# The third block of batch 0 in split float16, beside two blocks in float32

## The chip, the cores and the metric

One core of a Trainium2 chip runs the whole program. The metric is the device time of one execution in microseconds; the median of several executions is given, and one more execution is recorded by the hardware profiler. An engine is named by its profile name where rows are read: PE is TensorE (PEld its weight loads), DVE is VectorE, ACT is ScalarE, POOL is GpSimd, SP issues the DMAs.

## The reference

Attention over 4 batches, 8 heads, 1152 keys and head size 64, with queries averaged in pairs (576 of them), then two dense layers. In short:

```python
q_pool = q.reshape(B, H, S // 2, 2, D).mean(axis=3)
scores = scale * np.matmul(q_pool, k.transpose(0, 1, 3, 2))
attn = np.exp(scores - np.max(scores, axis=-1, keepdims=True))
attn = attn / (np.sum(attn, axis=-1, keepdims=True) + 1e-09)
x = np.matmul(attn, v)            # 4 x 8 x 576 x 64, heads joined to rows of 512
h = x @ w_in                      # 512 -> 2048
g = np.where(h >= 1, h, np.where(h <= -1, 0.0, (h + 1) ** 2 / 4))
y = g @ w_out                     # 2048 -> 512
h2 = np.maximum(np.maximum(y @ w1, y @ w2), y @ w3)   # 512 -> 768, three times
out = h2 @ w_o2                   # 768 -> 512
```

## The kernel before

Most products are made in float16 with each operand as a high and a low part (hi, lo), three matmuls for one: hi x hi, hi x lo, lo x hi. `split` makes the parts, the high one on GpSimd and the low one on VectorE; `root_scale` and `norm` find the power of two that scales them.

The attention runs over 48 units: 4 batches x 3 blocks of 192 queries (`i`) x 4 pairs of heads (`p`). In this text unit n is the n-th of them, from 0, so units 0 to 11 are batch 0 and units 8 to 11 its third block. A unit has three tiles of 128 rows by 1152 keys (`who` 0 and 1 for the two heads, 2 for the remaining 64 rows of both). For each tile `soft` makes scores on TensorE (`qk`, line 352), their maximum on VectorE (366) and the exponential with its sum on ScalarE (367, 368). `turned` brings the probabilities into the transposed tile `pt`, and `av` multiplies `pt` with v one unit later; `shares` brings the row sums into place (lines 379 to 388).

`WHOLE(b, p)` at line 38 says which units stay in float32; it is true for all of batch 0. In a float32 unit `turned` transposes all three tiles on TensorE (line 404, nine transposes a tile) and ScalarE evicts each to `pt` (415, 417); `av` uses float32 matmuls (435) on a float32 v. In a split unit tiles 0 and 1 are cast by ScalarE (421), subtracted by VectorE (422) and transposed by a DMA from SP (423); only tile 2 goes over TensorE, evicted by ScalarE (410) and VectorE (411); `av` uses three times the matmuls in float16 (440).

The order on TensorE is written out by hand: `ORDER` is a list of words for a unit, one list for float32 units and one for split units. s is `soft` of a tile, t `turned`, r `shares`, a1 the `av` of the unit before, q `q_prep` of the next pair of units, d a step of the dense part, w a step that prepares w_in and w_out. The float32 list puts q ahead of the third tile and `av` behind the second t; the split list puts `av` ahead of the third tile and q behind it. Dense steps start with unit 6: in four words d there are two up steps (line 506) and one down step (532), the down step of a block running while the next block's up steps run, so there is none before unit 10. What the other engines do is put in order by the scheduler of the language, by program order and its own estimate of time; each engine then runs its own queue in order, SP included.

k and v of a batch are prepared by `k_steps` and `v_steps` in steps that `put` ties to units (`K1` and `V1`: around the last units of the batch before): a load by SP into one of two buffers (`nat`), a square sum on ScalarE (line 266), then `split`, and for k a transpose by DMA (283). In batch 0 the float32 v is loaded straight into one of the four `vhl` buffers. The rest of the program (two weights, the dense part that is left, the last two layers) follows when the attention is over.

## Time and profile before

| | us |
|---|---|
| median of three runs | 1231.83 (1231.8 to 1234.66) |
| profiled execution | 1239.84 |
| its span, first to last instruction | 1237.9 |

Busy in the span: TensorE 1077.9 us (87%), VectorE 857.5 (69%), ScalarE 696.8 (56%), GpSimd 302.9 (24%). The rows below are of the profiled execution. A busy time of TensorE is a modelled one, as its matmuls are pipelined; a wait is named by what came last.

The stretches used below are cut at the first score matmul of a unit: unit 5 starts at 146.89 us, unit 8 at 200.03, unit 9 at 216.19, unit 10 at 231.74, unit 11 at 258.97, unit 12 at 279.70, unit 17 at 361.21, unit 20 at 405.51, unit 23 at 454.61, unit 24 at 473.50, unit 29 at 557.82, unit 32 at 602.88, unit 41 at 753.18.

### The profile page before, as it was taken

To read this page: it belongs to the slowest core of one execution; us is meant where nothing else is said; L and a number is where in the kernel's file an instruction comes from. 1 tells how busy PE (TensorE), PEld (TensorE's weight loads), DVE (VectorE), ACT (ScalarE), POOL (GpSimd) and SP (SyncE) were. 2 spreads that over 40 slices of the span, in tenths; PEclk is the share of its full clock that TensorE was granted. 3 is DMA by queue.
4 is the path that set the end of the run, shared out by engine and by line. 5 is a ranking of instruction groups with operands and counts; after the bars stand their busy time and mean duration, and the time that the engine had idled before them with its cause. 6 is when DMAs were issued, how large, how long until landed. Compare 5 with 4: busy or idle time off the path is not lost.

```text
span 1237.9 us, 26735 instructions
## 1 busy us (share of the span) xinstructions
PE 1077.9 (87%) x11058; PEld 881.2 (71%) x11058; DVE 857.5 (69%) x1454; ACT 696.8 (56%) x1241; POOL 302.9 (24%) x306
## 2 busy tenths in 40 slices
PE   0456788899999987999988899998697999999998
PEld 0334567677788876888877788887696876767774
DVE  3988765657888888988888988886988652322220
ACT  3868676656667777667776677766453411122111
POOL 1310012323222344322234422221643020100000
PEclk9867889999999999999999999999899999999999
DMA  9963211446766688965588766547433220000001
GB/s 289 267 199 106 90 27 26 84 87 155 129 113 120 109 172 170 167 110 110 110 158 177 146 105 107 97 88 157 160 96 117 90 67 18 10 27 18 17 18 43
DMA packets 273753, 134.90 MB, mean 109 GB/s; under 512 B 229088, under 2 KB 256736, under 8 KB 272608
## 3 DMA queue, kind: packets, MB, share of 16 engines
q1 hardware_dynamic: 273632, 133.20, 48.5%
q8 instruction: 86, 1.41, 0.5%
q14 instruction: 35, 0.29, 0.1%
HBM read 62.39 MB, written 9.44 MB: 58 GB/s over the span
## 4 chain that ended last, share of the span: by engine, by line
PE 41%; DVE 17%; issue 7%; DMA 7%; ACT 6%; POOL 4%; SPq 2%; ACTq 0%; POOLq 0%; DVEq 0%
PE p L752 17%; PE po L769 5%; PE ph L506 5%; PE py L532 4%; DVE st L366 4%; DMA qn<-in_q_dram 3%; PE sc L352 3%; PE tr L404 3%; PE av L440 2%; DVE g L517 2%; DVE hl L422 2%; DVE t L514 2%; ACT pf L368 1%; POOL g L515 1%; ACT hl L421 1%
## 5 line engine op out<-in xcount | busy, mean ns | idle before, releaser
L352 PE MATMUL sc<-kst,qst 128*64 128x512 f16 (+3 forms) x1152 | 178.2, 347 | 62.6 <-DMA qst<-qpre 21.1
L532 PE MATMUL py<-g,wou 128*128 128x192 f16 x2304 | 201.1, 248 | 22.4 <-POOL g L515 7.8
L752 PE MATMUL p<-yh,wm 128*128 128x288 f16 x1728 | 216.0, 287 | 3.7 <-ACT py L536 2.7
L532 PEld LDWEIGHTS <-wou 128*128 128x128 f16 x2304 | 191.3, 99 | 31.8 <-issue 31.4
L506 PE MATMUL ph<-xh,win 128*128 128x192 f16 x2304 | 203.2, 249 | 4.9 <-ACT py L536 2.6
L366 DVE TENSOR_REDUCE st<-sc 128x1 f32<-128x1152 f32 x144 | 194.1, 1348 | 18.0 <-PE sc L352 17.8
L752 PEld LDWEIGHTS <-wm 128*128 128x128 f16 x1728 | 169.6, 98 | 49.6 <-issue 4.4
L506 PEld LDWEIGHTS <-win 128*128 128x128 f16 x2304 | 195.1, 99 | 7.5 <-issue 5.7
L368 ACT ACTIVATE pf<-sc,st,esc 128x1152 f32<-128x1152 f32 x144 | 188.7, 1311 | 4.5
L352 PEld LDWEIGHTS <-qst 128*64 128x64 f16 (+1 forms) x1152 | 85.6, 109 | 124.3 <-issue 56.9
L513 POOL TENSOR_TENSOR rl<-t,rl 128x384 f32<-128x384 f32 x96 | 103.7, 1083 | 185.3 <-DVE rl L512 185.3
L404 PE MATMUL tr<-ident,pf 128*128 128x128 f32 x648 | 98.9, 306 | 26.3 <-ACT pf L368 17.4
L422 DVE TENSOR_TENSOR hl<-pf,hl 128x1152 f16<-128x1152 f32 x72 | 104.3, 1449 | 22.7 <-ACT hl L421 22.6
L404 PEld LDWEIGHTS tr<-ident,pf 128*128 128x128 f32 x648 | 83.5, 161 | 40.9 <-ACT pf L368 24.8
L367 ACT ACTIVATE st<-st,esc 128x1 f32<-128x1 f32 x144 | 41.6, 289 | 119.0 <-DVE st L366 118.8
L760 ACT ACTIVATE h<-mx 128x288 f16<-128x288 f32 x48 | 21.2, 442 | 133.3 <-DVE mx L758 133.3
L757 DVE TENSOR_TENSOR mx<-p,mx 128x288 f32<-128x288 f32 x48 | 21.9, 456 | 106.3 <-PE p L752 105.7
L515 POOL TENSOR_SCALAR g<-t,dgs 128x384 f16<-128x384 f32 x96 | 70.7, 738 | 97.0 <-DVE t L514 91.4
L440 PE MATMUL av<-pt,vhl 128*64 128x192 f16 x1944 | 87.1, 247 | 2.7 <-DMA pt<-hl 2.7
L440 PEld LDWEIGHTS <-vhl 128*64 128x64 f16 x1944 | 79.3, 110 | 12.4 <-issue 8.5
L517 DVE SCALAR_TENSOR_TENSOR g<-t,dgs,g 128x384 f16<-128x384 f32 x96 | 74.2, 781 | 16.4 <-POOL g L515 16.2
L421 ACT ACTIVATE hl<-pf 128x1152 f16<-128x1152 f32 x72 | 83.4, 1159 | 0.9
(169 smaller groups left out, 1339.0 us busy)
## 6 DMA issues: line engine op xcount, KB each, us to landing
kn<-in_k_dram SPq DMA_DIRECT2D x16, 576.0 KB, 4.6
vn<-in_v_dram SPq DMA_DIRECT2D x16, 576.0 KB, 5.0
raw_m<-in_moe_w_dram SPq DMA_DIRECT2D x12, 768.0 KB, 5.1
raw_in<-in_moe_w_in_dram SPq DMA_DIRECT2D x8, 1024.0 KB, 5.4
qn<-in_q_dram SPq DMA_DIRECT2D x24, 256.0 KB, 4.0
raw_ou<-in_moe_w_out_dram SPq DMA_DIRECT2D x10, 512.0 KB, 4.6
qst<-qst SPq DMA_DIRECT2D x48, 96.0 KB, 2.2
y_d<-ys SPq DMA_DIRECT2D x48, 96.0 KB, 2.0
```

Source lines behind the costliest of these rows:

```text
L352: nc.tensor.matmul(sc[m0:m1, n0:n1], qst[b, i, p][who][:, var, m0:m1], ks[:, h, n0:n1], start=(var == 0), stop=(var == 1))
L366: nc.vector.tensor_reduce(out=m, in_=sc, axis=AX.X, op=ALU.max, negate=True)
L368: nc.scalar.activation(out=pf, in_=sc, func=AF.Exp, bias=nb, scale=e, accum_out=sums[b, i, p][:, who:who + 1])
L404: nc.tensor.transpose(tr[:, c * P:(c + 1) * P], pf[:, c * P:(c + 1) * P], ident)
L421: nc.scalar.activation(out=hl[:, 0], in_=pf, func=AF.Copy)
L422: nc.vector.tensor_tensor(out=hl[:, 1], in0=pf, in1=hl[:, 0], op=ALU.subtract)
L440: nc.tensor.matmul(acc[64 * h:64 * h + 64], vhl[b, p][:, vi, h, c, :], pt[:, h, pi * KT + c, :], start=(c == 0 and e == 0), stop=(c == KT ...
L506: nc.tensor.matmul(ph[:, a], win[:, wi, kt, ff * P:(ff + 1) * P], x[:, xi, kt], start=(kt == 0 and e == 0), stop=(kt == KD - 1 and e == 2))
L513: nc.gpsimd.tensor_tensor(out=rl, in0=t2, in1=rl, op=ALU.add)
L517: nc.vector.scalar_tensor_tensor(out=g[:, 1, fs, :], in0=t2, scalar=gs, in1=g[:, 0, fs, :], op0=ALU.mult, op1=ALU.subtract)
L532: nc.tensor.matmul(py, wou[:, ff // 2, wi, ff % 2, m * P:(m + 1) * P], g[:, gi, ff, :], start=(ff == 0 and e == 0), stop=(ff == NF - 1 and ...
L752: nc.tensor.matmul(ph[:, :NB2], wm[:, wi, i, kt, ff * P:(ff + 1) * P], yh[:, yi, kt, n0:n0 + NB2], start=(kt == 0 and e == 0), stop=(kt == ...
```

## The change

`WHOLE` takes the block instead of the pair and is true for the first two blocks of batch 0 alone. So units 8 to 11 follow the split way in `turned`, in `av` and in `ORDER`. Their v is needed in two parts: a new generator `v_again` loads each pair's v of batch 0 a second time, into a `nat` buffer, and splits it into a `vhl` buffer, with the scale found before. Its load is tied to the third tile of units 4 to 7 and its split to the first tile of units 6 to 9. As v of block 2 is now scaled, the factor `Uv` of each pair is written again in that block.

```diff
--- before.py
+++ after.py
@@ -35,7 +35,7 @@
 DEPTH = 1
 DENSE = 6
 POOL_KV = False
-WHOLE = lambda b, p: b == 0
+WHOLE = lambda b, i: b == 0 and i < 2
 ORDERED = {mybir.EngineType.PE}
 
 
@@ -285,7 +285,7 @@
 
     def v_steps(b, p):
 
-        if WHOLE(b, p):
+        if WHOLE(b, 0):
             vn = stk.tile([P, 2, KT, D], F32, tag="vhl", name=f"vn{b}_{p}")
             load_q.dma_start(out=vn, in_=v[b, 2 * p:2 * p + 2].rearrange("h (p c) d -> p h c d", p=P))
             yield
@@ -300,6 +300,15 @@
         vv = vhl[b, p].rearrange("p e a b c -> p e (a b c)")
         yield from norm(vn, vv[:, 0], 1, b, p, "v")
         split(vv[:, 0], vv[:, 1], vn.rearrange("p a b c -> p (a b c)"), sb[b][:, p, 1:2])
+        yield
+
+    def v_again(p):
+
+        vn = load(v, 0, p, "v")
+        yield
+        vhl[0, p] = stk.tile([P, 2, 2, KT, D], F16, tag="vhl", name=f"vhl0_{p}")
+        vv = vhl[0, p].rearrange("p e a b c -> p e (a b c)")
+        split(vv[:, 0], vv[:, 1], vn.rearrange("p a b c -> p (a b c)"), sb[0][:, p, 1:2])
         yield
 
     def q_prep(b, i, p):
@@ -395,7 +404,7 @@
         if who == 0:
             PT[b, i, p] = ptp.tile([P, 2, 2 * KT, NB], F16, tag="pt", name=f"pt_{b}_{i}_{p}")
         pt = PT[b, i, p]
-        if who == 2 or WHOLE(b, p):
+        if who == 2 or WHOLE(b, i):
 
             tr = place(f"tr{key}")
             rs = tr[:, KT * P:KT * P + 2 * P]
@@ -404,7 +413,7 @@
                 nc.tensor.transpose(tr[:, c * P:(c + 1) * P], pf[:, c * P:(c + 1) * P], ident)
             if who == 2:
                 R[b, i, p] = rs
-            if not WHOLE(b, p):
+            if not WHOLE(b, i):
                 tr = tr.rearrange("p (c h q) -> p h c q", c=KT, h=2)
                 hi, lo = pt[:, :, 0:KT, P:NB], pt[:, :, KT:2 * KT, P:NB]
                 nc.scalar.activation(out=hi, in_=tr, func=AF.Copy)
@@ -428,23 +437,23 @@
         pt = PT.pop((b, i, p))
         bank = psg.tile([P, 512], F32, tag="g1", name=f"av{b}_{i}_{p}")
         acc = bank[:, :NB]
-        if WHOLE(b, p):
+        if WHOLE(b, i):
             pt = whole(pt)
             for c in range(KT):
                 for h in HO:
                     nc.tensor.matmul(acc[64 * h:64 * h + 64], vhl[b, p][:, h, c, :], pt[:, h, c, :],
                                      start=(c == 0), stop=(c == KT - 1))
-        for c in range(0 if WHOLE(b, p) else KT):
+        for c in range(0 if WHOLE(b, i) else KT):
             for e, (vi, pi) in enumerate(((0, 0), (0, 1), (1, 0))):
                 for h in HO:
                     nc.tensor.matmul(acc[64 * h:64 * h + 64], vhl[b, p][:, vi, h, c, :], pt[:, h, pi * KT + c, :],
                                      start=(c == 0 and e == 0), stop=(c == KT - 1 and e == 2))
         if p == 0:
             xf[b, i] = xp.tile([P, KD, NB], F32, tag="xf", bufs=1, name=f"xf{b}_{i}")
-        if i == 0:
-            if p == 0:
+        if i == 0 or (b == 0 and i == 2):
+            if p == 0 and i == 0:
                 Uv[b] = small.tile([P, NPAIR + 3], F32, tag="Uv", bufs=3, name=f"Uv{b}")
-            if WHOLE(b, p):
+            if WHOLE(b, i):
                 nc.vector.tensor_scalar(out=Uv[b][:, p:p + 1], in0=u_in[:, p:p + 1], scalar1=1.0, scalar2=None,
                                         op0=ALU.mult)
             else:
@@ -578,6 +587,11 @@
                 put(t + x, kg)
             for x in (V1 if b else V0[p]):
                 put(t + x, vg)
+
+    for p in range(NPAIR):
+        again = v_again(p)
+        for x in (2, 6):
+            put(3 * ((2 - 1) * NPAIR + p) + x, again)
 
     def now(t):
         for gen in events.get(t, ()):
@@ -625,7 +639,7 @@
                 wdue -= 1
 
     for n, (b, i, p) in enumerate(units):
-        for word in ORDER[WHOLE(b, p)].split():
+        for word in ORDER[WHOLE(b, i)].split():
             attend(n, word)
     last = len(units)
     turned(*behind.pop((last - 1, 2)))
```

## Rows read from the trace of the kernel before

**Rows 1.** The page's chain that ended last: shares of the span by engine.

```profile
PE 41%; DVE 17%; issue 7%; DMA 7%; ACT 6%; POOL 4%; SPq 2%; ACTq 0%; POOLq 0%; DVEq 0%
```

**Rows 2.** Windows of units 8 to 12: length, busy by engine, clock, DMA.

```profile
200.03:216.19 16.16, 14.09 (x139) 11.26 (x138) 7.97 (x16) 11.20 (x19) 3.69 (x4) 1.00 0.03 7
216.19:231.74 15.55, 14.18 (x142) 11.56 (x140) 10.07 (x21) 10.34 (x18) 7.12 (x8) 1.00 0.20 46
231.74:258.97 27.23, 22.71 (x192) 18.31 (x191) 16.04 (x33) 14.96 (x27) 6.43 (x8) 0.81 0.53 112
258.97:279.70 20.73, 18.36 (x191) 15.73 (x190) 11.93 (x23) 11.83 (x21) 6.80 (x7) 1.00 0.54 78
279.70:297.46 17.76, 15.85 (x175) 13.66 (x173) 12.83 (x20) 12.58 (x23) 5.81 (x6) 1.00 0.55 135
```

**Rows 3.** Timeline of units 8 and 10: start, us, instructions, idle time before.

```profile
201.58 1.20 PE L404 MATMUL tr<-ident,pf 128*128 128x128 f32 x9 [0.40 <-ACT pf L368]
...
239.14 1.16 ACT L266 ACTIVATE kpre<-kn 128x1152 bf16<-128x1152 f32 x1 [2.38 <-DMA kn<-in_k_dram]
...
240.31 1.29 ACT L368 ACTIVATE pf<-sc,st,esc 128x1152 f32<-128x1152 f32 x1
...
241.74 1.37 PE L352 MATMUL sc<-kst,qst 128*128 128x512 f16 x6 [2.98 <-ACT pf L368]
...
243.16 2.18 PE L404 MATMUL tr<-ident,pf 128*128 128x128 f32 x9
```

**Rows 4.** Windows of units 8 to 16, 20 to 28 and 32 to 40.

```profile
200.03:361.21 161.18, 144.41 (x1569) 122.08 (x1568) 114.77 (x205) 103.66 (x187) 52.28 (x55) 0.97 0.54 102
405.51:557.82 152.31, 136.84 (x1685) 119.56 (x1683) 131.22 (x219) 107.39 (x198) 55.05 (x55) 0.99 0.76 146
602.88:753.18 150.30, 136.61 (x1683) 119.39 (x1682) 129.78 (x219) 107.34 (x198) 53.87 (x54) 0.99 0.71 137
```

**Rows 5.** Groups of instructions by line: busy us, mean ns of one, idle before.

```profile
L532 PE MATMUL py<-g,wou 128*128 128x192 f16 x2304 | 201.1, 248 | 22.4 <-POOL g L515 7.8 <-DVE xf L453 7.6 <-DVE g L517 7.0
...
L422 DVE TENSOR_TENSOR hl<-pf,hl 128x1152 f16<-128x1152 f32 x72 | 104.3, 1449 | 22.7 <-ACT hl L421 22.6
...
L404 PE MATMUL tr<-ident,pf 128*128 128x128 f32 x648 | 98.9, 306 | 26.3 <-ACT pf L368 17.4 <-issue 4.4 <-ACT R L388 3.0
L440 PE MATMUL av<-pt,vhl 128*64 128x192 f16 x1944 | 87.1, 247 | 2.7 <-DMA pt<-hl 2.7
...
L421 ACT ACTIVATE hl<-pf 128x1152 f16<-128x1152 f32 x72 | 83.4, 1159 | 0.9
...
L411 DVE TENSOR_TENSOR pt<-tr,pt 128x1152 f16<-128x1152 f32 x36 | 48.8, 1355 | 10.5 <-ACT pt L410 10.5
...
L435 PE MATMUL av<-pt,vn 128*64 128x192 f32 x432 | 40.1, 342 | 0.0
...
L415 ACT ACTIVATE pt<-tr 128x1152 f32<-128x1152 f32 x24 | 27.1, 1129 | 21.4 <-PE tr L404 21.3
```

**Rows 6.** DMA issues of the page: count, KB each, median us to landing.

```profile
vn<-in_v_dram SPq DMA_DIRECT2D x16, 576.0 KB, 5.0
...
pt<-hl SPq DMA_TRANSPOSE x72, 4.8
```

**Rows 7.** Groups by line: the split of v in later batches.

```profile
L246 DVE SCALAR_TENSOR_TENSOR vhl<-vn,sb,vhl 128x1152 f16<-128x1152 f32 x12 | 21.1, 1758 | 11.5 <-POOL vhl L245 11.4
...
L245 POOL TENSOR_SCALAR vhl<-vn,sb 128x1152 f16<-128x1152 f32 x12 | 15.8, 1319 | 42.4 <-ACT t L511 14.8 <-DVE Uv L451 11.5 <-PE ph L506 9.3
```

**Rows 8.** Windows of unit 5 and of units 23 and 24.

```profile
146.89:164.50 17.61, 11.65 (x91) 8.37 (x90) 12.17 (x22) 11.40 (x20) 2.77 (x3) 0.90 0.23 47
454.61:473.50 18.89, 15.62 (x193) 13.51 (x191) 15.47 (x28) 12.50 (x24) 7.89 (x7) 1.00 0.98 189
473.50:493.38 19.88, 15.79 (x192) 13.57 (x190) 18.22 (x32) 14.85 (x27) 9.86 (x8) 1.00 0.75 170
```

**Rows 9.** Timeline at the start: the early load of batch 1's first v.

```profile
37.89 0.37 SPq L260 DMA_DIRECT2D vn<-in_v_dram  x1
```

## The prediction

> **What bounds the kernel now.** I read the chain of waits first [rows 1]: TensorE carries 41% of it, VectorE 17%, and no other engine has as much. So the order on TensorE sets the end, and what VectorE and ScalarE do counts where TensorE waits for them. Then I cut the span at the first score matmul of each unit. A unit is one batch, block and pair of heads; units 8 to 11 are the third block of batch 0, the one that changes, and unit 12 still holds the last float32 output sum of unit 11.
>
> The windows of units 8 to 12 [rows 2] differ widely. Units 8 and 9 take 16.16 and 15.55 us with 14 us of TensorE work: they hold two up steps of the dense part but no down step yet. Units 10 and 11 hold one down step more. Unit 11 takes 20.73 us, 18.36 of them TensorE; unit 10 takes 27.23 at a granted clock of 0.81, though it holds the same work. The reader should see in the timeline of unit 10 [rows 3] why: ScalarE, which runs its queue in order, sits 2.38 us in front of the square of the next k until its load lands; the exponential behind it starts only at 240.31, TensorE idles 2.98 us, and its next nine transposes take 2.18 us. In unit 8 the same nine take 1.20 us [rows 3]. That is the half clock (1.2 of 2.4 GHz), and the loss against unit 11 is 27.23 - 20.73 = 6.5 us.
>
> The best guide to the changed kernel is in this trace already: at the starts of batches 2 and 3 the same work (k and v of the next batch prepared beside the last block) runs with the split form of the probabilities. Units 8 to 16 take 161.18 us, units 20 to 28 152.31 and units 32 to 40 150.30 [rows 4].
>
> **The change, part by part.** Four units change, 8 to 11.
>
> *TensorE.* Each loses 18 of its 27 float32 transposes. By their group [rows 5] one costs 98.9 / 648 = 0.153 us, so 2.75 us. The float32 output sum costs 40.1 / 12 = 3.34 us, the split one 87.1 / 36 = 2.42 [rows 5], so 0.92 less. Together 3.7 us a unit, 14.7 in all; a part of these averages is half clock, so it is an upper figure.
>
> *ScalarE.* Three evictions of 1.13 us go, two casts of 1.159 us come and one eviction, counted like those [rows 5]: 3.4 us against 3.4, no change.
>
> *VectorE.* Two subtractions of 1.449 us and one of 1.355 are added [rows 5]: 4.25 us a unit, 17.0 in all. VectorE was the engine with room in these windows (8 to 16 us busy, [rows 2]). With it, units 8 to 16 hold 114.8 + 17.0 = 131.8 us of VectorE, and the two later stretches hold 131.22 and 129.78 [rows 4]; so they are a fair picture of the load.
>
> *SP and the DMA.* Two DMA transposes a unit are added, eight in all; the 72 that exist land in a median of 4.8 us [rows 6]. They have from the exponential of unit n to the output sum in unit n+1 to do so, about one unit. Behind them on SP stand the q loads and the copies of transposed q. I cost them at nothing, covered by the up steps of the next unit; without that cover the output sum would wait the remainder of 4.8 us. The trace's rows speak against a page here: the Trainium skill ("VectorE: DVE Perf Modes", section "The three transpose paths") gives 1309 ns for one 128x128 block by DMA against 390 ns on TensorE. An estimate from that page for the 18 blocks of one such transfer is 23.6 us, 188 us for eight, which would make the kernel far slower. The 4.8 us of the row decides: the blocks are not done one after the other.
>
> *The second v.* Four loads of 576 KB (5.0 us to land, [rows 6]) and four splits, each 1.319 us on GpSimd and 1.758 us on VectorE [rows 7]. They are programmed in units 4 to 9, the splits from unit 6 on. A split waits for its v buffer, which the float32 v leaves after the output sum of the block before; GpSimd runs in order, so additions of q and the dense part's g steps queue behind that wait, and TensorE's down steps read g. What a split puts on the path lies between 0 and its whole 1.76 us, 0 to 7.0 for four; it can't be a gain, being added work. VectorE is busy less than 75% in units 5, 8 and 9 [rows 2, 8], so I take a quarter, 1.8 us. The fold of the scale into Uv in units 9 to 12 is one small VectorE instruction in place of another: nothing.
>
> *The load buffers.* Now the two buffers for raw k and v hold the first k and v of batch 1 early; that v's load issues at 37.89 us [rows 9]. After the change reloads take them, and the first k and v of batch 1 must wait for the splits of the third and the fourth reload, in units 8 and 9. Both are squared in units 9 and 10, one unit after; landing needs 5.0 us. I take 0, with the price of a miss under the rivals.
>
> *Sum.* Replacing units 8 to 16 by the mean of the two later stretches: 161.18 - (152.31 + 150.30) / 2 = 161.18 - 151.3 = 9.9 us gained. This contains the end of unit 10's stall: in units 23 and 24 [rows 8] the clock is 1.00 and each takes under 20 us. Less 1.8 for the splits. The later stretches have a down step in all units, units 8 and 9 have none; 48 matmuls of 201.1 / 2304 [rows 5] make 4.2 us, 8.4 for two, but VectorE (14 to 16 us with its additions) rather than TensorE will be longest there, so I count 1.0 of it, between 0 and 8.4. Gain 9.9 - 1.8 + 1.0 = 9.1 us. With the bounds of the splits and the down steps it is 3.9 to 18. TensorE's order is fixed by hand, and what follows unit 16 is unchanged, so the gain reaches the end whole. The profiled execution took 1239.84 us (span 1237.9), so 1230.7 by its own time; the median of the runs is 8.0 lower, 1231.83, which gives **1222.7 us**, own range 1214 to 1228.
>
> **Rivals.**
> 1. *The stall stays, or one like it comes.* TensorE has only about 14 - 3.7 = 10.4 us of work in units 8 and 9 of some 15.5, and unit 5, with 11.65 of 17.61 us, ran at a clock of 0.90 [rows 8]. If the clock falls there, or the square of the late k stays ahead of the exponential, 6.5 us come back: 9.1 - 6.5 = 2.6 gained, 1229.2. Against it: units 23 and 24 have the same loads and no drop. The Trainium skill ("TensorE: Matmul & The Clock Gate", section "HAM oscillation — how this bites in real kernels") says that an array waiting between bursts goes back to half clock and starts the next burst cold. Rows 3 agree (2.18 us after the wait); by that rule thinning TensorE's work is itself a risk.
> 2. *Slower: the ring of two load buffers.* The first k and v of batch 1 land too late, ScalarE stands in front of their squares as it does in unit 10 now, and TensorE falls to half clock each time. Each costs 6.5 us as in unit 10. With both new ones and the old one kept: 9.1 - 3 x 6.5 = -10.4, 1242.2. It turns slower from the second. Against it: one unit of lead, against 5.0 us to land. For it: SP and GpSimd run in order, so a late split delays the load.
> 3. *More than forecast.* Units 8 and 9 fall towards TensorE's own work and half of the 8.4 us counts: 9.9 + 4.2 = 14.1, 1217.7.
> 4. *Nothing to gain in ordinary runs.* The profiled execution is 8.0 us above the median. If that is unit 10's stall and the like, runs without a profile lack it, and VectorE's 17 us use up the rest: 0 to 2 us, 1231.
>
> **How the numbers follow.** Forecast 0.55, rival 1 0.20, rival 2 0.12, rival 3 0.08, rival 4 0.05. About 0.3% (3.7 us) is what a measurement of this kernel can tell from no change. Faster by more: forecast, rival 3 and a fifth of rival 1 (a cheaper stall), 0.67. Within it: the rest of rival 1 and rival 4, 0.21. Slower: rival 2, 0.12. The range leaves out rival 2 and the far end of rival 3: 1215 to 1232.
>
> **What would show it.** Right: units 8 to 16 in about 152 us, no window of them below a clock of 0.95, units 10 and 11 at 16 to 19 us, VectorE busy about 135 us in the stretch. Rival 1: a window of units 8 to 12 at 0.9 or below, with ScalarE waiting for a k or v load in front of it. Rival 2: two or three such waits. Rival 3: units 8 and 9 under 14 us. Wrong altogether: the stretch as long as before with the clock at 1.00, which would mean that VectorE took over what TensorE gave; or a loss after unit 16, which I took as unchanged.

## The result, and the profile after

The changed kernel takes 1239.6 us (median; 1235.92 to 1240.62) against 1231.8 for the kernel before, a ratio of 1.0057 with an interval of 1.0036 to 1.0077. It is slower; the forecast was 1222.7, and the range ended at 1232. In a second sitting the same compiled program (e7 below) took 1.0017 of the kernel before (1.0001 to 1.0034), so the loss is 0.2 to 0.6%. The profiled execution of the first sitting took 1238.76 us with a span of 1237.0.

The base first. The kernel before was run once more, unchanged (e1): 1234.35 us, ratio 0.9997, span 1232.3, while the execution in front of the prediction had a span of 1237.9. Below, "the kernel before" in a comparison by stretches is this second execution, which lies near its median. By it the change does this: units 0 to 5 +0.3 us, units 6 and 7 together **+7.7**, units 8 to 16 **-5.0**, units 17 to 46 -0.5, and +2.3 from unit 47 to the end, together +4.7. Executions of one program differ by some of this. Two of the runs below have edits that left the compiled order as it was, so that e6 is a third execution of the kernel before and e7 a second one of the changed kernel:

| us in units | kernel before, three executions | changed kernel, two executions |
|---|---|---|
| 0 to 5 | 162.8 to 164.5 | 163.1 and 164.7 |
| 6 and 7 | 33.3 to 35.5 | 41.2 and 38.0 |
| 8 to 16 | 159.7 to 161.6 | 154.7 and 154.3 |
| 17 to 46 | 476.8 to 479.1 | 476.3 and 477.3 |
| 47 to the end | 397.2 to 399.5 | 401.7 and 401.1 |

Three differences are larger than these spreads: units 6 and 7 are 2.5 to 7.9 us longer, units 8 to 16 are 5.0 to 7.3 us shorter, and the end is 1.6 to 4.5 us longer.

Windows of the changed kernel for units 6 to 12, in that order (start and end, length; busy time and instructions of TensorE, its weight load, VectorE, ScalarE, GpSimd; granted clock, DMA share, GB/s). The last five answer to [rows 2]:

```profile
163.09:186.22 23.13, 17.70 (x139) 13.69 (x138) 16.60 (x25) 16.74 (x24) 4.69 (x5) 0.78 0.11 34
186.22:204.27 18.05, 15.60 (x140) 12.37 (x138) 14.22 (x19) 10.82 (x19) 6.25 (x7) 0.91 0.28 76
204.27:217.22 12.95, 11.55 (x122) 9.33 (x121) 9.94 (x19) 8.51 (x16) 5.50 (x5) 1.00 0.37 90
217.22:234.16 16.94, 12.78 (x139) 10.68 (x139) 15.92 (x24) 11.38 (x21) 6.27 (x8) 0.90 0.55 125
234.16:257.33 23.17, 18.77 (x189) 16.27 (x189) 21.52 (x39) 16.47 (x28) 9.20 (x8) 0.85 0.76 157
257.33:273.83 16.50, 15.11 (x193) 13.37 (x191) 14.34 (x20) 10.33 (x20) 8.11 (x7) 1.00 0.97 203
273.83:295.50 21.67, 17.00 (x191) 14.86 (x190) 18.78 (x35) 15.35 (x27) 7.11 (x8) 0.92 0.79 160
```

Units 8 and 11 run at a clock of 1.00 in 12.95 and 16.50 us, against 16.16 and 20.73 in [rows 2]. Units 9, 10 and 12 are below it (0.90, 0.85, 0.92), and unit 12 has grown from 17.76 to 21.67 us. Unit 6, where the first of the new splits stands, takes 23.13 us at 0.78 (19.98 in the execution ahead of the prediction).

The same columns for the second execution of the kernel before: units 6 and 7 in one window, units 8 to 16, and unit 10.

```profile
162.84:196.29 33.45, 27.99 (x275) 22.49 (x274) 25.31 (x41) 27.86 (x42) 9.55 (x11) 1.00 0.09 22
196.29:355.99 159.70, 144.02 (x1569) 122.09 (x1568) 114.85 (x205) 102.20 (x184) 53.57 (x55) 0.97 0.51 103
227.38:254.75 27.37, 22.65 (x192) 18.34 (x191) 16.03 (x33) 15.05 (x28) 6.62 (x8) 0.81 0.53 112
```

Units 6 and 7 take 33.45 us there at a clock of 1.00. Unit 10 is as long as in [rows 2], so its stall belongs to the kernel and not to one execution.

The changed kernel's units 6 and 7 in one window, then units 8 to 16, 20 to 28 and 32 to 40, as in [rows 4]:

```profile
163.09:204.27 41.18, 33.30 (x277) 26.06 (x275) 30.82 (x44) 27.57 (x42) 10.94 (x12) 0.83 0.19 52
204.27:358.98 154.71, 133.96 (x1569) 116.07 (x1568) 135.07 (x222) 104.80 (x189) 58.07 (x57) 0.96 0.72 144
403.06:554.66 151.60, 136.32 (x1683) 119.30 (x1682) 131.94 (x219) 107.44 (x198) 56.24 (x55) 0.99 0.76 146
599.37:748.16 148.79, 136.02 (x1684) 119.35 (x1683) 131.10 (x219) 107.18 (x198) 52.79 (x54) 0.99 0.72 139
```

Units 6 and 7 take 41.18 us at 0.83. Units 8 to 16 fell from 161.18 (159.70 in the second execution) to 154.71, not to about 151; VectorE holds 135.07 us in it. The two later ones are what they were.

Groups by line and DMA issues of the changed kernel, which answer to [rows 5] and [rows 7] (busy us, mean ns of one; idle before):

```profile
L431 DVE TENSOR_TENSOR hl<-pf,hl 128x1152 f16<-128x1152 f32 x80 | 115.4, 1443 | 26.5 <-ACT hl L430 26.5
...
L413 PE MATMUL tr<-ident,pf 128*128 128x128 f32 x576 | 87.0, 304 | 33.1 <-ACT pf L377 21.8 <-issue 4.6 <-ACT R L397 4.4
L449 PE MATMUL av<-pt,vhl 128*64 128x192 f16 x2160 | 96.7, 247 | 3.9 <-DMA pt<-hl 3.9
...
L246 DVE SCALAR_TENSOR_TENSOR vhl<-vn,sb,vhl 128x1152 f16<-128x1152 f32 x16 | 27.5, 1720 | 8.0 <-POOL vhl L245 7.9
...
L245 POOL TENSOR_SCALAR vhl<-vn,sb 128x1152 f16<-128x1152 f32 x16 | 21.6, 1352 | 54.8 <-ACT t L520 23.0 <-PE ph L515 10.0 <-PE av L444 7.6
```

The DMA issues, as in [rows 6] (KB of each, median us to landing):

```profile
vn<-in_v_dram SPq DMA_DIRECT2D x20, 576.0 KB, 4.6
...
pt<-hl SPq DMA_TRANSPOSE x80, 4.7
```

A transpose, an output sum, a subtraction and a landing cost what they cost before. The split of v (lines 245 and 246) has four more instructions on each engine and nearly the same mean (1352 ns against 1319 on GpSimd, 1720 against 1758 on VectorE). What changed is where they stand.

**Where units 6 and 7 go.** The timeline of unit 6 in the changed kernel (start, us, engine, line, instruction, idle time before and what ended it) is one chain through four queues:

```profile
161.63 0.38 POOL L230 PARTITION_ALL_REDUCE U_ou<-um_ou  x1 [6.85 <-DVE um_ou L96]
...
168.81 1.22 POOL L245 TENSOR_SCALAR vhl<-vn,sb 128x1152 f16<-128x1152 f32 x1 [6.80 <-issue]
...
170.06 1.42 DVE L246 SCALAR_TENSOR_TENSOR vhl<-vn,sb,vhl 128x1152 f16<-128x1152 f32 x1 [2.24 <-POOL vhl L245]
...
171.40 1.28 DVE L148 SCALAR_TENSOR_TENSOR wou<-wou,s_ou 128x1024 f16<-128x1024 f32 x1
...
172.71 1.15 ACT L147 ACTIVATE wou<-wou,s_ou 128x1024 f16<-128x1024 f32 x1 [2.13 <-DVE wou L148]
...
173.77 0.56 ACT L520 ACTIVATE t<-ph,hh 128x384 f32<-128x384 f32 x1
...
174.23 0.32 ACT L396 ACTIVATE R<-tr 128x192 f32<-128x192 f32 x1
174.58 0.22 ACT L397 ACTIVATE R<-tr 64x64 f32<-64x64 f32 x1
...
174.85 2.18 PE L413 MATMUL tr<-ident,pf 128*128 128x128 f32 x9 [3.09 <-ACT R L397]
```

GpSimd starts the first half of pair 0's split at 168.81. VectorE has the second half at the head of its queue, and has been idle for 2.24 us when GpSimd is done. Behind it on VectorE stands a second half of the split of w_out (line 148, 171.40), for which ScalarE waits 2.13 us with the next first half (line 147); behind that stand ScalarE's copies of R; and TensorE waits 3.09 us for those and runs its nine transposes at half clock, 2.18 us as in the stalled unit 10 of [rows 3] against 1.20. In e7, the second execution, the chain is the same: GpSimd starts at 169.35, the waits are 2.71, 2.52 and 3.40 us, and the nine transposes take 2.18.

GpSimd's 6.80 us ahead of the split wait for nothing that the profile shows ("issue"). The instruction before it in GpSimd's queue is the partition all-reduce that finds the scale of w_out (line 230). Its own row lasts 0.38 us, but in all twenty traces of this document GpSimd starts nothing for at least 6.7 us after the end of a row of a partition all-reduce. The kernel before shows it too (7.12 us here, in e1, and 7.03 in the execution ahead of the prediction), where an addition of q comes next:

```profile
159.08 0.38 POOL L230 PARTITION_ALL_REDUCE U_ou<-um_ou  x1 [5.84 <-issue]
166.57 0.98 POOL L321 TENSOR_TENSOR qn<-qn 128x384 f32<-128x384 f32 x1 [7.12 <-issue]
```

So the compiler put the first split right behind an instruction that most likely holds GpSimd for about 7 us. No run moves the all-reduce, so this is argued from the rows and not tested.

### The profile page after: what moved, and what is told of

Same layout as the page of the kernel before. It is cut to its first block, busy times and chain, and to the rows that moved or that the text cites. A ratio compares the mean times of both kernels' runs of the same rounds, so it can differ in the third digit from the quotient of the medians.

```text
span 1237.0 us, 26819 instructions
## 1 busy us (share of the span) xinstructions
PE 1068.9 (86%) x11058; PEld 876.3 (71%) x11058; DVE 884.4 (71%) x1474; ACT 696.2 (56%) x1241; POOL 313.6 (25%) x310
## 3 DMA queue, kind: packets, MB, share of 16 engines
q8 instruction: 86, 1.41, 0.5%
## 4 chain that ended last, share of the span: by engine, by line
PE 44%; DVE 22%; DMA 10%; ACT 9%; issue 9%; POOL 4%; SPq 2%; ACTq 0%; POOLq 0%; DVEq 0%
PE p L766 17%; PE py L541 6%; DVE st L375 5%; PE po L783 5%; PE sc L361 5%; PE ph L515 4%; PE av L449 3%; PE tr L413 3%; DVE hl L431 2%; DMA qn<-in_q_dram 2%; DVE g L526 2%; ACT pf L377 2%; DMA kn<-in_k_dram 2%; DVE t L523 2%; ACT hl L430 2%
## 5 line engine op out<-in xcount | busy, mean ns | idle before, releaser
L541 PE MATMUL py<-g,wou 128*128 128x192 f16 x2304 | 207.4, 252 | 26.8 <-DVE xf L462 12.0
L541 PEld LDWEIGHTS <-wou 128*128 128x128 f16 x2304 | 197.4, 101 | 36.7 <-issue 35.6
L522 POOL TENSOR_TENSOR rl<-t,rl 128x384 f32<-128x384 f32 x96 | 108.7, 1135 | 172.5 <-DVE rl L521 171.7
L431 DVE TENSOR_TENSOR hl<-pf,hl 128x1152 f16<-128x1152 f32 x80 | 115.4, 1443 | 26.5 <-ACT hl L430 26.5
L413 PE MATMUL tr<-ident,pf 128*128 128x128 f32 x576 | 87.0, 304 | 33.1 <-ACT pf L377 21.8
L376 ACT ACTIVATE st<-st,esc 128x1 f32<-128x1 f32 x144 | 41.7, 289 | 128.8 <-DVE st L375 128.3
L413 PEld LDWEIGHTS tr<-ident,pf 128*128 128x128 f32 x576 | 73.4, 159 | 46.0 <-ACT pf L377 28.7
L449 PE MATMUL av<-pt,vhl 128*64 128x192 f16 x2160 | 96.7, 247 | 3.9 <-DMA pt<-hl 3.9
L449 PEld LDWEIGHTS <-vhl 128*64 128x64 f16 x2160 | 88.1, 110 | 14.6 <-issue 9.7
L430 ACT ACTIVATE hl<-pf 128x1152 f16<-128x1152 f32 x80 | 92.6, 1158 | 0.9
```

The costliest lines, as they stand in the source:

```text
L413: nc.tensor.transpose(tr[:, c * P:(c + 1) * P], pf[:, c * P:(c + 1) * P], ident)
L430: nc.scalar.activation(out=hl[:, 0], in_=pf, func=AF.Copy)
L431: nc.vector.tensor_tensor(out=hl[:, 1], in0=pf, in1=hl[:, 0], op=ALU.subtract)
L449: nc.tensor.matmul(acc[64 * h:64 * h + 64], vhl[b, p][:, vi, h, c, :], pt[:, h, pi * KT + c, :], start=(c == 0 and e == 0), stop=(c == KT ...
L522: nc.gpsimd.tensor_tensor(out=rl, in0=t2, in1=rl, op=ALU.add)
L541: nc.tensor.matmul(py, wou[:, ff // 2, wi, ff % 2, m * P:(m + 1) * P], g[:, gi, ff, :], start=(ff == 0 and e == 0), stop=(ff == NF - 1 and ...
```

## The experiments

All ratios are against the kernel before, run on the same chip in the same sitting. The quoted expectations name theories by letters and say in each what they hold.

**e1: the kernel before again.** No edit.

> The kernel before, unchanged, profiled a second time. Its first profiled execution took 1239.84 us, 8.0 above the median of its timed runs. Theory A (the 8 us were the stall of unit 10 and its half clock, which ordinary executions don't have): this profile has a span near 1230 and unit 10 takes at most 22 us at a clock of 0.95 or more. Theory B (unit 10's stall belongs to the kernel, the 8 us lay elsewhere): unit 10 takes 26 us or more here too, and the ratio is 1.000.

Measured: 1234.35 us, 0.9997 (0.9975 to 1.0019). Unit 10 is 27.37 us at 0.81 again.

**e2: v split from the copy on the chip, no second load.**

```diff
-        vn = load(v, 0, p, "v")
+        vn = vhl[0, p]
-        ... stk.tile([P, 2, 2, KT, D], F16, tag="vhl", name=f"vhl0_{p}")
+        ... stk.tile([P, 2, 2, KT, D], F16, tag="vhl", bufs=5, name=f"vhl0_{p}")
-        rb = tp.tile([P, 3, 64], F32, tag="rb", bufs=2, ...
+        rb = tp.tile([P, 3, 64], F32, tag="rb", bufs=1, ...
```

> The changed kernel without the second load of v: the split parts are made from the float32 v that is on chip, in a fifth v buffer (one row-sum buffer is given up for the room), so the two load buffers keep the first k and v of batch 1 as before. The same splits, the same units in split form. Theory C (the reload's hold on the two load buffers and its place in the queues cost the time): 4 to 8 us below the changed kernel, ratio 0.997 to 1.001. Theory D (the split form of units 8 to 11 itself gains nothing over ordinary executions of before, as VectorE and a thin TensorE take the gain): within 2 us of the changed kernel, ratio 1.004 to 1.008.

Measured: 1239.6 us, 1.0037 (1.0020 to 1.0054). Units 6 and 7 take 37.3 us, units 8 to 16 155.2, units 17 to 46 482.2 (476.8 in the kernel before). The whole is no faster without the second load, but it holds two further changes: pair 0's split now ran at 36.2 us already, and some 5 us were lost after unit 16, which e8 and e16 show too (484.5 and 483.1). They share with e2 the fifth v buffer and the row-sum buffer given up for it; which of the two costs this was not tested. What the second load costs is read from e12.

**e3: the second load and split alone.** Batch 0 stays float32 throughout; the second split goes into a spare buffer. The edit is to the kernel before.

```diff
+    def v_again(p):
+
+        vn = load(v, 0, p, "v")
+        yield
+        spare = hlp.tile([P, 2, 2, KT, D], F16, tag="hl", name=f"vhl0_{p}")
...
```

> The kernel before with the second load and the split of v added, into buffers whose content nothing reads; all of batch 0 stays in float32. Theory C: most of the loss is here, ratio 1.004 to 1.008, units 4 to 9 longer by 4 to 8 us in sum. Theory D: the four splits are 12 us of GpSimd and VectorE beside other work, ratio 0.999 to 1.002.

Measured: 1241.81 us, 1.0048 (1.0028 to 1.0069). Nothing holds these splits back: they run from 52.6 to 127 us, beside the work on w_in and w_out. Units 0 to 5 end at 171.1 us in place of 162.8, units 6 and 7 take 33.6. So the same loads and splits cost some 8 us where they meet the work on the weights, here earlier than in the changed kernel. The spare buffer is one of the ring `hl`, so a part of this may be the order of the other engines (see e13).

**e4: TensorE's order of batch 0 kept in the third block.**

```diff
-        for word in ORDER[WHOLE(b, i)].split():
+        for word in ORDER[b == 0].split():
```

> The changed kernel, with units 8 to 11 following the word list of the float32 units (q ahead of the third tile, the output sum at the end). Theory D with the order as its part (the split list puts the output sum before its DMA transposes have landed): 2 us or more below the changed kernel. Otherwise within 2 us, ratio 1.004 to 1.008.

Measured: 1237.77 us, 1.0017 (0.9997 to 1.0038). Units 6 and 7 41.7, units 8 to 16 155.5: as in the changed kernel. The two words of the order are not the cause. The ratio is below 1.0057, but it is that of the changed kernel in e7.

**e5: the split form alone.** No second load, no second split; the output sums of units 8 to 11 read two slices of the split w_in in place of v. e10, e12 and e14 do the same.

```diff
-    for p in range(NPAIR):
-        again = v_again(p)
-        ...
+        vs = vhl[b, p]
+        if b == 0 and i == 2:
+            vs = win.rearrange(...)[:, :4 * KT * D].rearrange(...)
```

> This kernel makes the third block of batch 0 split and transposed by DMA, but neither loads nor splits v a second time: the output sums of these four units read two slices of the split w_in in place of a split v (so these four results are not the reference's). Theory A (the second load and the v splits, which fall among the last splits of w_out in units 6 and 7, cost the time, and the split form itself gains): units 2 to 7 back at 108 to 111 us (116.1 in the changed kernel, 108.1 in the kernel before), units 8 to 16 at 152 to 155, the whole at 1224 to 1229 us. Theory D (VectorE and a thinner TensorE eat what the split form frees): units 8 to 16 at 158 or more, the whole at 1232 to 1236. Theory E (the order of ScalarE's and VectorE's queues, which the compiler chooses anew, costs time in places that the change does not touch): units 2 to 16 as in theory A, but 3 us or more lost after unit 16, the whole at 1230 to 1235.

Measured: 1235.77 us, 1.0008 (0.9984 to 1.0032). Units 8 to 16 take 154.5 us, as in the whole change, so the split form does gain 5 to 7 us there. But units 6 and 7 take 37.5 us, 2 to 4 more than in the kernel before, although nothing was added to them. ScalarE's queue shows why something moved: the square of batch 1's first k, the 57th of ScalarE's activations in the trace of the kernel before (91.4 us), is the 165th here (214.2 us); the expectations of e13 and e14 count it as place 53 and 159. Its target comes from the ring `hl`, and the casts of unit 8 take buffers of that ring first.

**e6 and e7: the square of the next k queued one tile later**, in the kernel before and in the changed one.

```diff
-K1 = (-2, 0, 2)
+K1 = (-2, 1, 2)
```

> The kernel before with one number changed: the square of each next batch's k is queued one tile later, one tile ahead of its split in place of two, so that its load has two tiles to land as v's has. If the stall of unit 10 is ScalarE standing on that load: unit 10 falls from 27.4 us to about 20 at a clock of 0.95 or more, units 8 to 16 from 159.7 to 152 to 155, the whole to 1225 to 1229 us. If the wait only moves to the square of v or to the split: unit 10 stays above 25 us or another unit takes it up, the whole at 1231 to 1235.

Measured: 1234.44 us, 1.0004 (0.9984 to 1.0023). The edit tested nothing: the square still ran at 234.91 us (234.86 in e1), behind a wait of 2.12 us (2.26), and every engine's trace has the same instructions in the same order as in the kernel before. The compiler places the square by its own reckoning.

> The changed kernel with the same one number changed. If the half-clock stretches that it keeps in units 9, 10 and 12 (16.9, 23.2 and 21.7 us) are ScalarE standing on late k loads: these three fall to 15 to 19 us each, units 8 to 16 from 154.7 to about 147 to 150, units 2 to 7 stay at 114 to 117, the whole falls from 1239.6 to 1232 to 1236 us. If they come from VectorE, which is busy 16 to 22 us in them: no change in units 8 to 16 (153 to 156), the whole at 1237 to 1241.

Measured: 1237.2 us, 1.0017 (1.0001 to 1.0034). Units 9, 10 and 12 take 17.2, 22.1 and 17.1 us (16.9, 23.2, 21.7), unit 11 takes 20.4 (16.5), and the stretch stays at 154.3. But here, too, the traces of ScalarE, VectorE, GpSimd and SP agree with the changed kernel's instruction by instruction, so neither theory was tested. What it shows is how far two executions of one program differ: units 9 and 10 have low clocks again, the third falls into unit 11 in place of 12, and units 6 and 7, one window each, take 38.0 us in place of 41.2:

```profile
164.70:185.53 20.83, 16.21 (x140) 12.92 (x138) 15.58 (x20) 14.57 (x22) 4.67 (x5) 0.84 0.10 31
185.53:202.71 17.18, 14.02 (x139) 11.25 (x138) 13.29 (x21) 11.36 (x18) 6.24 (x7) 1.00 0.29 79
```

**e8: e2 with the splits queued behind those of w_out.**

```diff
-        for x in (2, 6):
+        for x in (2, (12, 10, 8, 7)[p]):
```

> The kernel without reload (v split from the copy on the chip, 1239.6 us, units 2 to 7 in 112.3, units 8 to 16 in 155.2) with the four v splits queued later: all from the first tile of unit 8 on, behind the last splits of w_out, in place of one in each of units 6 to 9. Theory A (collision with the splits of w_out): units 6 and 7 fall to 15.6 to 18 us each, units 2 to 7 to 108 to 109, units 8 to 16 rise by 2 us at most, the whole at 1234 to 1237 us. Theory E (the order chosen anew costs the time, wherever the splits stand): units 2 to 7 change by less than 2 us, or what they give is lost elsewhere; the whole at 1238 to 1242.

Measured: 1240.63 us, 1.0040 (1.0017 to 1.0063), units 6 and 7 38.3. It tested nothing, as e6: the splits ran at 168.6 and 186.2 us all the same, and the order on ScalarE, VectorE, GpSimd and SP is that of e2, of which this is a second execution.

**e9 to e11: ScalarE's and VectorE's order kept as programmed**, in the kernel before, in e5 and in the changed kernel.

```diff
-ORDERED = {mybir.EngineType.PE}
+ORDERED = {mybir.EngineType.PE, mybir.EngineType.Activation, mybir.EngineType.DVE}
```

> The kernel before with ScalarE's and VectorE's instructions, too, kept in the order in which the program issues them (as TensorE's already are), up to the last layers. It is the base for the next two runs; only its difference to them counts. All theories: the order in which the program is written puts the work on the weights at the end of each unit, so units 0 to 7 get longer, the whole somewhere between 1235 and 1290 us; unit 10 shows whether a stall on the load of k is there as well.

> As the run before, but with the third block of batch 0 split and transposed by DMA (no second load or split of v; two slices of the split w_in stand in for the split v, so these four results are not the reference's). Theory E (the split form alone gained nothing in the whole because the compiler chose a new order for ScalarE and VectorE, which cost some 3 us in units 2 to 7): with the order kept, units 2 to 7 agree with the fixed kernel before within 1 us, units 8 to 16 are 4 to 8 us shorter, and the whole is 4 to 8 us shorter than that kernel. Theory F (units 2 to 7 vary between executions, order or not, and the gain in units 8 to 16 is that of the late stall): the whole within 2 us of that kernel, or units 2 to 7 differ by 2 us or more at the same order.

> The whole change (second load and split of v with it) with ScalarE's and VectorE's order kept as programmed. Theory E: units 2 to 7 rise over the two fixed kernels only by what the reload itself does, at most the four splits of 1.76 us on VectorE (0 to 7 us), and the whole lies 0 to 6 us below the fixed kernel before. Theory C (what hurts is that the second loads take the two load buffers from the first k and v of batch 1): units 8 to 12 show ScalarE or VectorE waiting for late k or v loads, and units 8 to 16 gain less than in the run before by 3 us or more; the whole is as long as the fixed kernel before or longer.

Measured: 2051.8, 2074.0 and 2078.6 us (1.6635, 1.6815, 1.6852). The base left the range that was meant, and at this order the split form lengthens units 8 to 16 from 274.6 to 301.9 us. Nothing follows for the tuned kernel but that the order of these two queues is worth 800 us of it, so an edit that moves it is not a local one. Units 2 to 7 agree within 1.3 us between the first two.

**e12: second loads without splits.** One column of each load is read in place of its split.

```diff
-        split(vv[:, 0], vv[:, 1], vn.rearrange(...), sb[0][:, p, 1:2])
+        nc.vector.tensor_scalar(out=one, in0=vn[:, 0, 0, 0:1], scalar1=1.0, ...)
```

> The split form of the third block with the second loads of v in their place, but with one column of each read in place of its split (the split w_in stands in for the split v, so four results are not the reference's). It lies between the split form alone (1235.8 us, units 2 to 7 in 112.5) and the whole change (1239.6, 116.1). Theory C (the loads' hold on the two buffers costs the time): units 2 to 7 at 115 to 117, the whole at 1238 to 1240 us. Theory A' (the splits do it, on GpSimd and VectorE among the last splits of w_out): units 2 to 7 at 111 to 113.5, the whole at 1234 to 1237 us.

Measured: 1229.78 us, 0.9969 (0.9945 to 0.9992): faster than the kernel before. Against the changed kernel only the splits are gone (and the order that goes with them), and units 6 and 7 take 34.13 us in place of 41.18 (38.01 in e7), at a clock of 0.95 in place of 0.83, while units 8 to 16 stay at 154.5. The window of units 6 and 7:

```profile
158.59:192.72 34.13, 29.66 (x276) 23.59 (x274) 27.05 (x44) 28.62 (x44) 10.19 (x11) 0.95 0.13 30
```

So in units 6 and 7 the second loads cost next to nothing; the splits do, or the order that goes with them, which differs here in many rows before unit 8. That the whole is faster than the kernel before comes in good part from elsewhere: units 0 to 5 take 158.6 us (162.8 in e1).

**e13: the moved square alone, in the kernel before.** Two buffers of the ring `hl` are taken in unit 8.

```diff
+                if key in ((8, 0), (8, 1)):
+                    pin = hlp.tile([P, 2 * KT * D], F16, tag="hl", ...)
+                    nc.vector.tensor_scalar(out=pin[:, 0:1], in0=item[4][:, 0:1], ...)
```

> The kernel before with one thing of the change alone: in unit 8 two buffers of the ring hl are taken (one column of the probabilities is copied into each), as the split form's casts take them. ScalarE's square of the first k of batch 1, which takes a buffer of that ring too, can then no longer run ahead in unit 2 and moves behind unit 8 (from place 53 of ScalarE's queue to place 159), and the compiler orders the rest anew, up to unit 7 nearly as in the split form alone. Theory E (this new order costs the time in units 2 to 7): units 2 to 7 in 111.5 to 114 us in place of 108.1, the whole at 1237 to 1241 us. Rival (units 2 to 7 vary by themselves): the whole within 2 us of the kernel before in the same session, units 2 to 7 at 107.5 to 111.

Measured: 1235.09 us, 1.0013 (0.9993 to 1.0033). The window of unit 6 of e5:

```profile
162.97:182.82 19.85, 16.67 (x139) 13.10 (x138) 14.34 (x22) 15.91 (x24) 4.13 (x4) 0.83 0.04 9
```

And of e13:

```profile
162.22:182.08 19.86, 16.68 (x140) 13.11 (x138) 14.27 (x21) 15.93 (x24) 4.13 (x4) 0.83 0.05 10
```

Units 2 to 6 of the two agree within 0.1 us, though e13 has no split form at all: the order before unit 8 is set by this one square. Units 6 and 7 take 36.4 us in e13, 3.0 more than in e1 and 0.9 more than in the execution ahead of the prediction, and units 8 to 16 give 2.1 of it back. The whole is not told from no change, so the size of this effect stays open.

**e14: the split form with the square put back** (the first k of batch 1 loaded and squared five tiles earlier).

```diff
-            for x in (K1 if b else K0[p]):
+            for x in ((-5, -4, 2) if b == 1 and p == 0 else K1 if b else K0[p]):
```

> The split form alone (no second v; the split w_in stands in for the split v, so four results are not the reference's), with the first k of batch 1 loaded and squared five tiles earlier in the program, ahead of unit 8's casts: the square is back at place 53, and ScalarE's order is that of the kernel before up to the last splits of w_out. Theory E: units 2 to 7 back at 107.5 to 110 us (112.5 without this), units 8 to 16 at 153 to 155.5, the whole at 1228 to 1232 us, faster than the kernel before by 0.2 to 0.5%. Rival (the split form gains nothing even so): the whole at 1233.5 to 1237 us.

Measured: 1232.99 us, 0.9984 (0.9961 to 1.0006). It can't be told from e5 (1.0008; the intervals overlap), and the stretches are not those of theory E: units 6 and 7 fell only from 37.5 to 35.8, and units 8 to 16 rose to 157.5.

**e15: the second split on GpSimd alone.**

```diff
-        split(vv[:, 0], vv[:, 1], vn.rearrange(...), sb[0][:, p, 1:2])
+        nc.gpsimd.tensor_scalar(out=vv[:, 0], in0=x, scalar1=s, ...)
+        nc.gpsimd.tensor_scalar(out=x, in0=x, scalar1=s, ...)
+        nc.gpsimd.tensor_tensor(out=vv[:, 1], in0=x, in1=vv[:, 0], op=ALU.subtract)
```

> The whole change with the second v split on GpSimd alone (its second half by a scaling in place and a subtraction there, nothing on VectorE). ScalarE's order stays that of the changed kernel but for a row or two, VectorE's too but for the four steps taken out. Theory A' (the VectorE half of the splits stands among the last splits of w_out and the dense steps in units 6 to 8): units 6 and 7 together fall from 41.2 to 36 to 38.5 us, units 2 to 7 to 111.5 to 114, the whole from 1239.6 to 1233 to 1236.5 us. Rival (what a split costs is the change of order, not VectorE's time): units 6 and 7 at 40 to 42 us, the whole at 1237.5 to 1241. Third case: GpSimd's longer steps hold up the dense part's g steps behind them; units 8 to 10 get longer by 2 us or more, 1240 or above.

Measured: 1246.47 us, 1.0106 (1.0065 to 1.0146). The order on ScalarE is the changed kernel's but for a few rows, VectorE is relieved of its halves, and units 6 and 7 rise to 43.4. So VectorE's time for its half is not what a split costs. The timeline of unit 6:

```profile
169.49 1.22 POOL L312 TENSOR_SCALAR vhl<-vn,sb 128x1152 f16<-128x1152 f32 x1 [7.54 <-PE ph L518]
...
172.11 2.37 POOL L314 TENSOR_TENSOR vhl<-vn,vhl 128x1152 f16<-128x1152 f32 x1
...
174.45 0.99 POOL L525 TENSOR_TENSOR rl<-t,rl 128x384 f32<-128x384 f32 x1
...
175.47 0.56 DVE L526 SCALAR_TENSOR_TENSOR t<-t,rl 128x384 f32<-128x384 f32 x1 [5.97 <-POOL rl L525]
...
177.26 1.15 ACT L147 ACTIVATE wou<-wou,s_ou 128x1024 f16<-128x1024 f32 x1 [4.89 <-DVE wou L148]
...
178.44 1.13 ACT L427 ACTIVATE pt<-tr 128x1152 f32<-128x1152 f32 x1
...
179.62 2.13 PE L364 MATMUL sc<-kst,qst 128*64 128x512 f16 x12 [5.99 <-ACT pt L427]
```

The dense part's addition (line 525) stands behind the three steps of the split on GpSimd until 174.45; VectorE waits 5.97 us for it, with the split of w_out (line 148) behind; ScalarE waits 4.89 us for that; TensorE waits 5.99 for ScalarE's eviction. It is the chain of the changed kernel with a longer first link; GpSimd starts 7.54 us after the all-reduce here.

**e16: copy on the chip, GpSimd alone, square early**, the three edits above in one kernel.

> All that theories E and A' ask for, as a complete kernel: v split from the copy on the chip (fifth v buffer, no second load), on GpSimd alone, and the first k of batch 1 loaded and squared five tiles earlier. If E and A' hold: units 2 to 7 in 107.5 to 110 us, units 8 to 16 in 153 to 156; units 20 to 28 may keep the 3.7 us that the fifth buffer cost in the kernel without reload; the whole at 1229 to 1234 us. If they don't: 1236 to 1241.

Measured: 1239.43 us, 1.0041 (1.0020 to 1.0061). Units 6 and 7 take 34.6 us, but units 2 to 5 78.3 (74.6 in e1) and units 17 to 46 483.1, a price that e2 shows as well.

**e17 and e18: the second split without GpSimd**, its first half on ScalarE (e17) or both halves on VectorE (e18). Load, place in the program and all else are the changed kernel's.

```diff
-        split(vv[:, 0], vv[:, 1], vn.rearrange(...), sb[0][:, p, 1:2])
+        split_rows(vv[:, 0], vv[:, 1], vn.rearrange(...), sb[0][:, p, 1:2])      # e17
+        nc.vector.tensor_scalar(out=vv[:, 0], in0=x, scalar1=s, ...)             # e18
+        nc.vector.scalar_tensor_tensor(out=vv[:, 1], in0=x, scalar=s, in1=vv[:, 0], ...)
```

> The whole change with the first half of the four v splits on ScalarE instead of GpSimd (the second half stays on VectorE). The queues of ScalarE and VectorE keep their order but for a few places. Theory H (VectorE stands in front of the split's second half until GpSimd, whose queue runs in order, has done the first, and the splits of w_out, ScalarE's evictions and TensorE stand behind that): units 6 and 7 together fall from 41.2 to 36 to 38.5 us, the whole from 1239.6 to 1232 to 1236 us. Rival (it is the added work beside the splits of w_out, whoever does it; ScalarE is as full there): units 6 and 7 at 39.5 us or more, the whole at 1237 to 1243.

Measured: 1235.05 us, 1.0013 (0.9998 to 1.0027). Up to the end of unit 6 ScalarE and VectorE have the changed kernel's order, with the one row added on ScalarE. Units 6 and 7, one window each, 33.63 us together (its profiled execution, 1239.8, lies above its median; the rest of it is not read):

```profile
164.04:180.64 16.60, 13.87 (x139) 11.26 (x138) 15.20 (x18) 15.31 (x23) 3.48 (x4) 1.00 0.13 40
180.64:197.67 17.03, 13.96 (x139) 11.25 (x138) 13.87 (x22) 12.58 (x21) 4.08 (x5) 1.00 0.26 72
```

> The whole change with both halves of the four v splits on VectorE. It takes GpSimd out too, but adds some 1.3 us a split to VectorE, and moves more of the order (44 rows of ScalarE, 114 of VectorE). Theory H: units 6 and 7 at 36.5 to 39 us, the whole at 1233 to 1237. Rival (added work on an engine that is full beside the splits of w_out): units 6 and 7 at 40 us or more, the whole at 1238 to 1244.

Measured: 1231.13 us, 0.9978 (0.9957 to 0.9999). It is complete and the fastest of the complete kernels. Units 6 and 7, 33.74 us together:

```profile
163.82:179.81 15.99, 13.96 (x139) 11.25 (x138) 14.58 (x20) 13.31 (x21) 4.55 (x4) 1.00 0.14 44
179.81:197.56 17.75, 15.58 (x139) 12.38 (x138) 16.61 (x27) 13.53 (x22) 6.79 (x6) 0.90 0.24 67
```

Both bring units 6 and 7 from 41.18 us (38.01 in e7) to 33.6 and 33.7, what they take in e1, with the same two splits in them. Nearly all of it comes in unit 6: 23.13 and 20.83 us in the changed kernel, 16.60 and 15.99 here. Unit 7, where the second split stands, hardly differs (18.05 and 17.18 against 17.03 and 17.75). What ScalarE waits for ahead of the first halves of w_out's split shows it, first in the groups by line of the changed kernel:

```profile
L147 ACT ACTIVATE wou<-wou,s_ou 128x1024 f16<-128x1024 f32 x7 | 8.0, 1144 | 5.8 <-DVE wou L148 5.8
```

Then in the groups by line of e18, with its own two halves of v:

```profile
L147 ACT ACTIVATE wou<-wou,s_ou 128x1024 f16<-128x1024 f32 x7 | 8.0, 1145 | 0.0
...
L313 DVE SCALAR_TENSOR_TENSOR vhl<-vn,sb,vhl 128x1152 f16<-128x1152 f32 x4 | 5.6, 1409 | 0.0
...
L312 DVE TENSOR_SCALAR vhl<-vn,sb 128x1152 f16<-128x1152 f32 x4 | 3.5, 870 | 0.0
```

5.8 us of waiting for VectorE are gone, though VectorE now does both halves; in e17 1.2 us are left, and the kernel before has 1.4. In e18 the first half starts at 164.46, in e17 at 164.42, in the changed kernel on GpSimd at 168.81: v and its buffer were there 4 us before GpSimd began, so they are not what it waited for.

## Why the prediction was wrong

**The splits of v, 1.8 us within 0 to 7.0: the step that failed.** The bound was "0 and its whole 1.76 us" for each, VectorE's busy time [rows 7]. Measured, unit 6 takes 20.83 to 23.13 us with the first half of its split on GpSimd and 15.99 to 16.60 without (e18, e17), so this one split costs 4.2 to 7.1 us by these executions, where 0.44 was counted for it and 1.76 was the bound. Not all of that is surely its own: e5 and e13 have no split, the changed kernel's order up to the end of unit 6 (but for two or three rows of VectorE's), and a unit 6 of 19.85 us at a clock of 0.83, and against them the price is 1.0 to 3.3 us. What the split adds in any case is the wait. In front of the nine transposes TensorE waits 3.09 and 3.40 us in the two executions of the changed kernel; in e5 and then in e17 the same rows are:

```profile
172.49 2.16 PE L413 MATMUL tr<-ident,pf 128*128 128x128 f32 x9 [0.84 <-ACT R L397]
```

```profile
172.10 1.20 PE L413 MATMUL tr<-ident,pf 128*128 128x128 f32 x9 [0.77 <-ACT R L397]
```

So 2.3 to 2.6 us are waiting, and the rest is the half clock, which e5 has after the shorter wait and e17 hasn't; why was not found. The split in unit 7 shows no such price. In the whole, e18 lies at 0.9978, below both measurements of the changed kernel (1.0057 and 1.0017, 4.8 to 9.7 us by the medians); e17 at 1.0013 is below the first alone. Two errors made it. First the unit: the lower value was argued from VectorE's room in units 5, 8 and 9 [rows 2, 8], but the program put splits from unit 6 on, and units 6 and 7, where the last splits of w_out alternate between ScalarE and VectorE, were not looked at. Second the kind of price: the bound counted the time in which the instruction runs, and what counted was the wait in front of it. GpSimd came to its half some 7 us after a partition all-reduce, which the text doesn't mention; VectorE stood 2.24 us before its own half began, everything in order behind it stood too, and then TensorE ran at half clock. The text named the queue behind GpSimd, even the dense steps in it, and then priced only VectorE.

The Trainium skill ("SBUF — State Buffer", section "SBUF: two separate sides") says that GpSimd and VectorE share a pair of ports, which GpSimd and a VectorE instruction with two inputs in SBUF (or in a two-port mode) lock against each other: the one that starts first holds it for its whole instruction, while the other is blocked. Rows of the changed kernel's unit 6 fit it, where line 148, 1.28 us elsewhere, runs beside an addition on GpSimd:

```profile
177.26 1.30 POOL L522 TENSOR_TENSOR rl<-t,rl 128x384 f32<-128x384 f32 x1 [0.93 <-DVE rl L521]
...
177.62 2.02 DVE L148 SCALAR_TENSOR_TENSOR wou<-wou,s_ou 128x1024 f16<-128x1024 f32 x1
```

That is 0.7 us, and e17 has the same 2.02 us; the waits in the chain are longer and are those of the queues.

**Units 8 to 16, 9.9 us by the later stretches.** The direction and the load were right (VectorE 135.07 us, about 135 was forecast; the DMA transposes land in 4.7 us and cost nothing), the size was not: 5.0 to 7.3 us by the executions at hand, where 9.9 and 1.0 for the down steps were counted. (The lower bound of the sum was also taken wrongly: with both terms at their lowest, 9.9 - 7.0 is 2.9 and not 3.9.) "This contains the end of unit 10's stall" was the failing part. The stall of unit 10 shrank from 27.2 to 23.17 us and others came in units 9 and 12. In units 9 and 10, at clocks of 0.90 and 0.85, ScalarE waits 0.83 us at most for a load, but 3.23 us for a maximum of VectorE, which is busy 15.92 of 16.94 and 21.52 of 23.17 us there. At the end of unit 11 it stands in front of a late v and in unit 12 of a late k:

```profile
232.38 0.29 ACT L376 ACTIVATE st<-st,esc 128x1 f32<-128x1 f32 x1 [3.23 <-DVE st L375]
...
272.43 1.16 ACT L266 ACTIVATE vhl<-vn 128x1152 bf16<-128x1152 f32 x1 [3.98 <-DMA vn<-in_v_dram]
...
285.52 1.16 ACT L266 ACTIVATE kpre<-kn 128x1152 bf16<-128x1152 f32 x1 [3.04 <-DMA kn<-in_k_dram]
...
288.12 1.17 PE L361 MATMUL sc<-kst,qst 128*64 128x512 f16 x12 [2.92 <-ACT R L397]
```

The late loads are the sign of rival 1; a full VectorE in units 9 and 10 is another explanation, and no run separates the two. In e7, the same program, unit 11 has a low clock in place of unit 12, and the stretch is as long. What the later stretches have and this one hasn't was not found: e5 has no second loads, waits up to 3.05 us for a k and takes 154.5 as well, so the second loads are not the cause.

**"What follows unit 16 is unchanged, so the gain reaches the end whole."** After unit 16 this held to unit 46 (476.3 and 477.3 against 476.8 to 479.1 us). What the text left out is that the order changes before unit 8: the hand-written order is TensorE's alone, and the compiler orders ScalarE and VectorE anew. e13 shows that taking two buffers of the ring `hl` in unit 8 moves a square from unit 2 behind unit 8 and with it the order of units 2 to 7. How much of the loss in units 6 and 7 is this is open: 1 to 4 us by e5 and e13, none by e12, e17 and e18, which have the late square too and take 33.6 to 34.1 us. As e17 has e5's order up to the end of unit 6, but for its own two rows and two more of VectorE's, it is hardly the order alone that sets the low clock there. Open is also the 1.6 to 4.5 us from unit 47 to the end.

**The rivals.** Rival 2 ended on the right side with 1242.2, for another reason: three late loads are not what made the kernel slow, for e12 has them (ScalarE waits 2.59, 2.38 and 3.59 us for a k) and is the fastest of all. Of rival 3's sign one half came, unit 8 in 12.95 us, but unit 9 took 16.94. Rival 4 fell with e1: unit 10's stall is there in an execution near the median. That the profiled execution lay 8 us above the median was spread over other units (unit 6 alone 2.1).

**What was right.** That units 10 and 11 hold the same work and the loss between them is a stall; the price of the float32 transposes and the sums; that the DMA transposes are covered, and in units 6 and 7 the second loads (e12).

## What to carry to other kernels

Price added work at the place where it will stand, and price a two-engine step by the chain of in-order queues behind each half: here 1.2 us on a GpSimd that is 24% busy made TensorE wait 2.3 to 2.6 us longer where it stood behind a partition all-reduce, and with the half clock behind the wait cost up to 7.1; the same work on ScalarE or on the busier VectorE cost none of that. Where only one engine's order is written by hand, every new claim on a shared ring of buffers is a change to the other engines' order, so compare their order before and after first; the compiled program shows it when an early instruction moves behind a hundred others. A stall that is known in the trace is not gained by removing the unit it stands in, unless what it waits for arrives earlier. And before reading what an edit did, see in the trace that the compiled order changed: three edits here left it as it was, and their runs are repeats, which are worth having, since executions of one program differed by 3 us in two units.
